# Half-empty operands moved from the streamed side to the loaded side of the matmuls, and a reordered start, in an attention-then-FFN kernel

## Chip, cores, metric

One core of a Trainium2 chip. The metric is the device time of one execution in microseconds (us). A profiled execution also has a span, from the first to the last instruction; it is about 1.7 us shorter than the time of that same execution (232.2 of 233.95 us before). The granted clock is the share of full rate at which PE was allowed to run.

PE is the matmul engine, PEld its weight loads, DVE the vector engine, ACT the scalar engine, POOL the GpSimd engine. A bank is one of the buffers in which PE leaves its sums; in this kernel DVE or ACT copies a sum out before its bank is used again. Silu is the activation h * sigmoid(h), done on ACT.

## The reference

Linear attention with decay over blocks, then a two-layer FFN with Silu. The inputs q, k, v are (4 batches, 8 heads, 768 positions, 64 dims), float32; the FFN is 512 to 2048 to 512 over 3072 tokens.

```python
for b in range(nb):                                   # blocks along the sequence
    intra = (qb @ kb^T) * Dmask;  intra = intra @ vb  # inside the block
    inter = (qb * lam_pow) @ kv_state                 # from all blocks before it
    out[block] = intra + inter
    kv_state = lam_block * kv_state + (kb * rev_pow)^T @ vb
x = out as tokens x 512
h = x @ w_in;  result = (h * sigmoid(h)) @ w_out
```

The kernel works in chunks of 128 positions (the reference's blocks have 64), 6 per batch, 24 in all; chunks 0, 6, 12 and 18 begin a batch and have no state.

## The kernel before

Two heads are packed in the 128 partitions (a "pair"; 4 pairs). A head has only 64 dims, so one operand of each product that contracts over dims must be zero for the other head. Before, the padded operand is the query, which streams through PE (`qt`, 256 columns per pair, half of them zeros).

```python
def st_t(c):                        # chunks 0 to 7: transposes on PE
    first = c < GROUPS[0] // BLK    # chunks 0 to 3
    tp = psum.tile([128, 2, NP, BLK], BF16, tag="o" if first else "att", ...)  # one bank for q and k
    ... 4 transposes of qb into tp[:, 0], 4 of kb into tp[:, 1] ...
    nc.vector.tensor_copy(qt[0:64, :, 0, :], tp[0:64, 0, :, :])
    nc.vector.tensor_copy(qt[64:128, :, 1, :], tp[64:128, 0, :, :])
    kt = tp[:, 1]                   # on ACT if first, else on DVE

def st_d(c):                        # state update
    vcast(c)                        # ACT: v to bf16
    ... 4 matmuls of 128 columns into kv; one 128x512 copy kv -> kvs ...

def st_s(c):                        # scores
    for half in range(2):
        for j in range(2):          # 256 streamed columns a pair
            nc.tensor.matmul(sp[:, 2*j:2*j+2, :], lhsT=kt[:, p, :], rhs=qt[:, p, :, :], ...)
        nc.vector.tensor_tensor(ss, sp, mask, op=AL.mult)

def st_o(c):                        # outputs
    for half in range(2):
        op = psum.tile([128, 2, 2, BLK], F32, tag="att", bufs=3)
        for j in range(2):          # 256 columns for each product
            nc.tensor.matmul(op[:, j, :, :], lhsT=pair_of(vb, p), rhs=res[half][:, 2*j:2*j+2, :], ...)
            if blk > 0:
                nc.tensor.matmul(op[:, j, :, :], lhsT=kvb[c][:, p, :], rhs=qt[:, p, :, :], ...)
        # of each [128, 2 heads] product only the two diagonal 64-row parts are wanted
        nc.scalar.activation(xt[g][0:64, ps, csl], op[0:64, :, 0, :], AF.Copy)
        nc.scalar.activation(xt[g][64:128, ps, csl], op[64:128, :, 1, :], AF.Copy)
```

So an output costs ACT four copies of 64x256, 0.38 us each in the trace. `ffn1(g, m)` is four matmuls of a group's columns into one of two `h` banks, which a Silu on ACT then empties; `ffn2` multiplies by `w_out`. After the start, `stretch(...)` interleaves `ffn1` tiles, `ffn2` parts and the pieces `t`, `d`, `s`, `o` of later chunks in a fixed order. One queue loads everything in order: chunks 0 to 3, `w_in` parts 0 to 3, chunk 4, `w_in` part 4, chunk 5, `w_out` parts. Each weight part is cast to bf16 on DVE before use.

## Time and profile before

| what | before |
|---|---|
| time, median of 3 (first measurement) | 234.6 us |
| span of the profiled run (its time: 233.95 us) | 232.2 us |
| PE busy | 209.8 us (90%) |
| ACT / DVE busy | 117.9 us (51%) / 81.3 us (35%) |
| start of the first output copy (DVE, `ob`) | 57.52 us |

The page of before: its heads, the busy time of each engine (us, share of the span, instructions), and the engines' shares of the chain that ended last.

```profile
span 232.2 us, 3510 instructions
...
PE 209.8 (90%) x1320; PEld 123.5 (53%) x1320; DVE 81.3 (35%) x130; ACT 117.9 (51%) x257; POOL 54.3 (23%) x60
...
PE 83%; ACT 7%; DVE 5%; issue 2%; DMA 1%; POOL 1%; ACTq 0%
```

PE bounds the kernel overall (90% of the span, 83% of the chain). Where it is back to back, time is the sum of the streamed columns: four products of 128, 256, 384 and 512 columns take 0.22, 0.44, 0.65 and 0.87 us in this trace. The timeline of before around one chunk's outputs (start us, length us, engine, line, operation, out<-in, partitions x elements, count):

```profile
119.44 0.27 PE L268 MATMUL op<-ss,vb 128*128 128x256 bf16 x1
119.54 0.27 PE L271 MATMUL op<-qt,kvs 128*128 128x256 bf16 x1
...
120.20 0.27 PE L271 MATMUL op<-qt,kvs 128*128 128x256 bf16 x1
120.31 0.81 PE L293 MATMUL h_ps<-xt,w_in_bf 128*128 128x384 bf16 x4
```

Read starts, not lengths: each of these products is 0.27 us long, but they start 0.10 to 0.11 us apart. The eight output products of 256 columns take 120.31 - 119.44 = 0.87 us.

The waits of PE in before, longest in total first (what waited, for what, total us, times, longest us):

```profile
PE tp L209 <- POOL qb L174: 6.7, 1, 6.7
PE sp L248 <- ACT kt L217: 4.1, 4, 1.6
PE kv_ps L232 <- ACT vb L191: 2.6, 3, 1.2
PE h_ps L293 <- ACT g L297: 1.9, 4, 0.7
```

In the start, scores wait for the key copy and the state update for the cast of v, both on ACT. Chunk 3 shows it, and what follows it:

```profile
21.47 0.61 PE L248 MATMUL sp<-qbd_99,kt 128*128 128x256 bf16 x4 [0.77 <-ACT kt L217]
...
23.29 0.38 PE L232 MATMUL kv_ps<-vb,kb 128*128 128x128 bf16 x4 [1.21 <-ACT vb L191]
...
27.43 7.93 PE L293 MATMUL h_ps<-xt,w_in_bf 128*128 128x512 bf16 x36 [0.25 <-ACT g L297]
```

The brackets give the idle time before and what ended it. On DVE, the cast of the last `w_in` part waits 5.03 us for its load, which lands at 33.7 us:

```profile
33.74 1.23 DVE L145 CAST w_in_bf<-w_tmp 128x2048 bf16<-128x2048 f32 x1 [5.03 <-DMA w_tmp<-in_moe_w_in_dram]
```

### The profile page before, as it was taken

To read this page: it belongs to the slowest core of one execution; us is meant where nothing else is said; L and a number is where in the kernel's file an instruction comes from. 1 tells how busy PE (TensorE), PEld (TensorE's weight loads), DVE (VectorE), ACT (ScalarE), POOL (GpSimd) and SP (SyncE) were. 2 spreads that over 40 slices of the span, in tenths; PEclk is the share of its full clock that TensorE was granted. 3 is DMA by queue.
4 is the path that set the end of the run, shared out by engine and by line. 5 is a ranking of instruction groups with operands and counts; after the bars stand their busy time and mean duration, and the time that the engine had idled before them with its cause. 6 is when DMAs were issued, how large, how long until landed. Compare 5 with 4: busy or idle time off the path is not lost.

```text
span 232.2 us, 3510 instructions
## 1 busy us (share of the span) xinstructions
PE 209.8 (90%) x1320; PEld 123.5 (53%) x1320; DVE 81.3 (35%) x130; ACT 117.9 (51%) x257; POOL 54.3 (23%) x60
## 2 busy tenths in 40 slices
PE   0465898899999988999999999999999999999993
PEld 0343545466555776666566555565666554444441
DVE  5378615740147533243224412430443310111121
ACT  5457665564403688567465554665466553433000
POOL 7661123025411223333333330333000000000000
PEclk9999999999999999999999999999999999999999
DMA  6999999999939998999999997999640100110212
GB/s 125 219 221 363 291 288 303 387 249 219 214 122 187 236 238 156 202 217 153 241 248 205 204 225 127 217 197 209 103 101 24 49 12 33 45 45 3 92 45 90
DMA packets 108849, 40.08 MB, mean 173 GB/s; under 512 B 101152, under 2 KB 102176, under 8 KB 108832
## 3 DMA queue, kind: packets, MB, share of 16 engines
q1 hardware_dynamic: 108688, 39.86, 77.4%
q8 instruction: 10, 0.16, 0.3%
q14 instruction: 7, 0.06, 0.1%
q10 hardware_dynamic: 144, 0.00, 0.0%
HBM read 27.27 MB, written 6.29 MB: 144 GB/s over the span
## 4 chain that ended last, share of the span: by engine, by line
PE 83%; ACT 7%; DVE 5%; issue 2%; DMA 1%; POOL 1%; ACTq 0%
PE o_ps L308 35%; PE h_ps L293 34%; PE sp L248 4%; PE op L268 4%; PE op L271 3%; PE kv_ps L232 2%; ACT xt L279 2%; ACT xt L278 2%; DMA lam_sb<-in_lam_dram 1%; ACT vb L191 1%; ACT kt L217 1%; PE tp L211 1%; ACT g L297 1%; DVE ss L251 1%; PE tp L209 1%
## 5 line engine op out<-in xcount | busy, mean ns | idle before, releaser
L293 PE MATMUL h_ps<-xt,w_in_bf 128*128 128x384 bf16 (+2 forms) x520 | 98.9, 323 | 2.6 <-ACT g L297 1.9
L297 ACT ACTIVATE g<-h_ps 128x384 bf16<-128x384 f32 (+2 forms) x128 | 62.3, 490 | 69.1 <-PE h_ps L293 68.2
L308 PE MATMUL o_ps<-w_out_bf,g 128*128 128x512 bf16 x384 | 94.9, 379 | 0.5 <-DVE w_out_bf L145 0.5
L293 PEld LDWEIGHTS <-w_in_bf 128*128 128x128 bf16 x520 | 50.3, 98 | 37.4 <-issue 3.9
L308 PEld LDWEIGHTS <-g 128*128 128x128 bf16 x384 | 37.3, 98 | 36.2 <-issue 0.7
L312 DVE COPY ob<-o_ps 128x512 f32<-128x512 f32 x24 | 16.6, 691 | 82.5 <-PE o_ps L308 82.5
L251 DVE TENSOR_TENSOR ss<-sp,mask 128x512 bf16<-128x512 f32 x48 | 30.9, 686 | 22.2 <-PE sp L248 22.0
L183 POOL TENSOR_TENSOR kb<-kf,lam_bwd 128x512 bf16<-128x512 f32 x24 | 25.0, 1042 | 4.2 <-DMA kf<-in_k_dram 2.4
L278 ACT ACTIVATE xt<-op 64x256 bf16<-64x256 f32 x44 | 16.5, 375 | 17.8 <-PE op L271 8.7
L268 PE MATMUL op<-ss,vb 128*128 128x256 bf16 x96 | 21.6, 277 | 0.2
L238 DVE CAST kvs<-kv_ps 128x512 bf16<-128x512 f32 x16 | 11.0, 688 | 24.7 <-PE kv_ps L232 24.7
L279 ACT ACTIVATE xt<-op 64x256 bf16<-64x256 f32 x44 | 16.6, 378 | 0.5
L174 POOL TENSOR_TENSOR qb<-qf,lam_fwd 128x512 bf16<-128x512 f32 x8 | 8.9, 1109 | 33.7 <-DMA qf<-in_q_dram 32.8
L248 PEld LDWEIGHTS <-kt 128*128 128x128 bf16 x96 | 8.8, 99 | 11.5 <-ACT kt L217 5.3
L191 ACT ACTIVATE vb<-vf 128x512 bf16<-128x512 f32 x24 | 14.8, 622 | 0.1
L271 PE MATMUL op<-qt,kvs 128*128 128x256 bf16 x56 | 13.1, 272 | 0.0
L177 POOL TENSOR_TENSOR qpad_107<-qf,lam_fwd 128x512 bf16<-128x512 f32 x5 | 5.2, 1042 | 27.1 <-DMA qf<-in_q_dram 23.3
L268 PEld LDWEIGHTS <-vb 128*128 128x128 bf16 x96 | 9.5, 100 | 2.9 <-issue 0.3
L177 POOL TENSOR_TENSOR qpad_109<-qf,lam_fwd 128x512 bf16<-128x512 f32 x6 | 6.3, 1042 | 20.0 <-DMA qf<-in_q_dram 12.6
L177 POOL TENSOR_TENSOR qpad_105<-qf,lam_fwd 128x512 bf16<-128x512 f32 x5 | 5.2, 1042 | 22.4 <-DMA qf<-in_q_dram 19.4
L232 PE MATMUL kv_ps<-vb,kb 128*128 128x128 bf16 x80 | 8.0, 223 | 2.6 <-ACT vb L191 2.6
L209 PE MATMUL tp<-ident,qb 128*128 128x128 bf16 x32 | 3.6, 242 | 6.7 <-POOL qb L174 6.7
(51 smaller groups left out, 82.4 us busy)
## 6 DMA issues: line engine op xcount, KB each, us to landing
qf<-in_q_dram SPq DMA_DIRECT2D x24, 256.0 KB, 3.7
kf<-in_k_dram SPq DMA_DIRECT2D x24, 256.0 KB, 4.3
vf<-in_v_dram SPq DMA_DIRECT2D x24, 256.0 KB, 4.5
out_dram<-ob SPq DMA_DIRECT2D x24, 256.0 KB, 2.3
w_tmp<-in_moe_w_out_dram SPq DMA_DIRECT2D x4, 1024.0 KB, 9.9
w_tmp<-in_moe_w_in_dram SPq DMA_DIRECT2D x3, 1024.0 KB, 7.8
w_tmp<-in_moe_w_in_dram SPq DMA_DIRECT2D x2, 512.0 KB, 5.5
kt<-kb SPq DMA_TRANSPOSE x16, 2.9
```

Source lines behind the costliest of these rows:

```text
L177: nc.gpsimd.tensor_tensor(qb[:, :, 0:4:3, :], qf.rearrange("s (p j) d -> s p j d", j=2), lam_fwd[:, blk, :].rearrange("s (p j) -> s p j", ...
L183: nc.gpsimd.tensor_tensor(kb, kf, lam_bwd[:, blk, :][:, :, None].to_broadcast([128, H, D]), op=AL.mult)
L191: nc.scalar.activation(natb[c][2], vraw.pop(c), AF.Copy)
L248: nc.tensor.matmul(sp[:, 2 * j:2 * j + 2, :], lhsT=kt[:, p, :], rhs=qt[:, p, :, :], start=True, stop=True)
L251: nc.vector.tensor_tensor(ss, sp, mask[:, None, :].to_broadcast([128, 4, BLK]), op=AL.mult)
L268: nc.tensor.matmul(op[:, j, :, :], lhsT=pair_of(vb, p), rhs=res[half][:, 2 * j:2 * j + 2, :], start=True, stop=(blk == 0))
L271: nc.tensor.matmul(op[:, j, :, :], lhsT=kvb[c][:, p, :], rhs=qt[:, p, :, :], start=False, stop=True)
L278: nc.scalar.activation(xt[g][0:64, ps, csl], op[0:64, :, 0, :], AF.Copy)
L279: nc.scalar.activation(xt[g][64:128, ps, csl], op[64:128, :, 1, :], AF.Copy)
L293: nc.tensor.matmul(hp[:, a:z], lhsT=w_in_bf[:, ko, m * 128:(m + 1) * 128], rhs=xt[g][:, ko, a:z], start=(ko == 0 and a == 0), stop=(ko == ...
L297: nc.scalar.activation(gg, hp[:, :n], AF.Silu)
L308: nc.tensor.matmul(o, lhsT=gt[g, ko][:, mt * BLK:(mt + 1) * BLK], rhs=w_out_bf[:, ko, :], start=(ko == 0), stop=(ko == KO_OUT - 1))
```

## The change

The intent: pad the operand that is loaded as weights, not the one that streams. Values (`vpad`), keys (`ktbd`) and the state (`kvbd`) get zeroed halves, four buffers of each, cleared once; the query is dense. Then the state product of a pair needs 128 columns for both heads, all products of an output add up in one bank, and one copy takes it out. Scores go by even and odd heads to two banks. For the first four chunks, query and key transposes get banks of their own, so that ACT copies the query while DVE copies the key. Casts of v are issued ahead of the scores. (On PE the first chunks' transposes already stood ahead of the outputs of the chunk before.)

```diff
@@ scores: same columns, other split
-        for half in range(2):
-            for j in range(2):
-                nc.tensor.matmul(sp[:, 2*j:2*j+2, :], lhsT=kt[:, p, :], rhs=qt[:, p, :, :], ...)
+        for j in range(2):
+            for p in range(NP):
+                nc.tensor.matmul(sp[:, p, :], lhsT=kt[:, p, j, :], rhs=qt[:, p, :], start=True, stop=True)
@@ outputs: 8 x 256 columns become 12 x 128, one bank, one copy
+        op = psum.tile([128, NP, BLK], F32, tag="att", bufs=3)
+        terms = [(kvb[c][:, p, :], qt[:, p, :], p) for p in range(NP)] if blk > 0 else []
+        for j in range(2):
+            terms += [(vb[:, p, 2*j:2*j+2, :], res[j][:, p, :], p) for p in range(NP)]
+        for i, (lhsT, rhs, p) in enumerate(terms):
+            nc.tensor.matmul(op[:, p, :], lhsT=lhsT, rhs=rhs, start=(i == 0), ...)
+        if c < N0:                                   # chunks 0 to 3
+            nc.scalar.activation(xt[g][:, 0:2, csl], op[:, 0:2, :], AF.Copy)
+            nc.vector.tensor_copy(xt[g][:, 2:4, csl], op[:, 2:4, :])
+        else:
+            nc.scalar.activation(xt[g][:, :, csl], op, AF.Copy)
@@ state: two half copies into the padded tile (ACT for chunks 0 to 3, else DVE)
-        nc.vector.tensor_copy(kvs, kv)
+        for j in range(2):
+            half_copy(nc.scalar if c < N0 else nc.vector, ...)   # 64x256 each
@@ keys of later chunks arrive dense by transposing DMA, then two DVE copies spread them
+    def spread_k(c): ...
@@ start
-    for c in range(4):
-        prep(c); st_t(c)
-        if c > 0: st_o(c - 1)
-        if c == 3: cast_w("in", 0)
-        st_s(c), st_d(c)
-    cast_w("in", 1)
-    ffn1(0, 0, 0), ffn1(0, 1, 0); st_o(3)
-    ffn1(0, 0, 1), ffn1(0, 1, 1); cast_w("in", 2); ...; ffn1(0, 2), ffn1(0, 3)
+    for c in range(N0):
+        prep(c); st_tq(c); st_tk(c)                  # own banks: tags "o" and "h"
+        if c > 0: st_o(c - 1)
+        vcast(c)
+        if c == N0 - 1: cast_w("in", 0)
+        st_s(c)
+        if c == N0 - 1: cast_w("in", 1)
+        st_d(c)
+    ffn1(0, 0, 0), ffn1(0, 1, 0); st_o(N0 - 1)
+    ffn1(0, 2, 0, tag="o"), ffn1(0, 3, 0, tag="o")
+    for m in range(4): ffn1(0, m, 1)
@@ ... chunks 4 and 5: transposes, casts and tiles slightly reordered; w_out casts in two halves (cut)
```

More of the change, by code (lines that the diff above doesn't have):

```diff
@@ L75, with clear @@
     )
-    NQBD = 3
-    qbd, qpad = [], []
-    for i in range(NQBD):
-        t = const.tile([128, NP, 2, BLK], BF16, name=f"qbd{i}")
-        nc.vector.memset(t, 0.0)
-        qbd.append(t)
-    for i in range(NQBD):
-        t = const.tile([128, NP, 4, D], BF16, name=f"qpad{i}")
-        nc.gpsimd.memset(t, 0.0)
-        qpad.append(t)
+    NKV = 4
+    vpad, ktbd, kvbd = [], [], []
+    for i in range(NKV):
+        vpad.append(const.tile([128, NP, 4, D], BF16, name=f"vpad{i}"))
+        ktbd.append(const.tile([128, NP, 2, BLK], BF16, name=f"ktbd{i}"))
+        kvbd.append(const.tile([128, NP, BLK], BF16, name=f"kvbd{i}"))
+    def clear(i):
+        nc.vector.memset(vpad[i], 0.0)
+        nc.vector.memset(ktbd[i], 0.0)
+        nc.vector.memset(kvbd[i], 0.0)
     log_lam = const.tile([128, H], F32)
@@ L92 @@
     nc.vector.tensor_copy(iota_f, iota_i)
+    clear(0)
+    clear(1)
     lam_exp = const.tile([128, NB, H], F32)
@@ L99 @@
     )
+    clear(2)
+    clear(3)
     lam_fwd = const.tile([128, NB, H], F32)
@@ L140, in cast_w @@
             dst = w_out_bf[:, a:z, :]
-        if which == "in" and i < 2:
+        if which == "in" and i == 0:
             nc.vector.tensor_copy(dst[:, 0:2, :], t[:, 0:2, :])
             nc.scalar.activation(dst[:, 2:4, :], t[:, 2:4, :], AF.Copy)
-        else:
-            nc.vector.tensor_copy(dst, t)
+        elif which == "in":
+            nc.vector.tensor_copy(dst, t)
+        else:
+            nc.vector.tensor_copy(dst[:, 0:2, :], t[:, 0:2, :])
+            nc.vector.tensor_copy(dst[:, 2:4, :], t[:, 2:4, :])
     raw, natb, tr, st, kvb, kvps = {}, {}, {}, {}, {}, {}
@@ L156 @@
     xt = {}
+    N0 = GROUPS[0] // BLK
     def load_c(c):
@@ L167, in load_c, with decay @@
         raw[c] = (qf, kf, vf)
+    def decay(table, blk):
+        return table[:, blk, :].rearrange("s (p j) -> s p j", j=2)[:, :, :, None].to_broadcast([128, NP, 2, D])
     def prep(c):
@@ L171, in prep @@
         qf, kf, vf = raw.pop(c)
-        if c < NPET:
-            qb = nat.tile([128, H, D], BF16, tag="qb")
-            nc.gpsimd.tensor_tensor(qb, qf, lam_fwd[:, blk, :][:, :, None].to_broadcast([128, H, D]), op=AL.mult)
-        else:
-            qb = qpad[c % NQBD]
-            nc.gpsimd.tensor_tensor(
-                qb[:, :, 0:4:3, :], qf.rearrange("s (p j) d -> s p j d", j=2),
-                lam_fwd[:, blk, :].rearrange("s (p j) -> s p j", j=2)[:, :, :, None].to_broadcast([128, NP, 2, D]),
-                op=AL.mult)
-        kb = nat.tile([128, H, D], BF16, tag="kb")
-        vb = nat.tile([128, H, D], BF16, tag="vb")
-        nc.gpsimd.tensor_tensor(kb, kf, lam_bwd[:, blk, :][:, :, None].to_broadcast([128, H, D]), op=AL.mult)
+        qb = nat.tile([128, NP, 2, D], BF16, tag="qb")
+        nc.gpsimd.tensor_tensor(qb, qf.rearrange("s (p j) d -> s p j d", j=2), decay(lam_fwd, blk), op=AL.mult)
+        kb = nat.tile([128, NP, 2, D], BF16, tag="kb")
+        nc.gpsimd.tensor_tensor(kb, kf.rearrange("s (p j) d -> s p j d", j=2), decay(lam_bwd, blk), op=AL.mult)
         vraw[c] = vf
-        natb[c] = (qb, kb, vb)
+        natb[c] = (qb, kb, vpad[c % NKV])
     vraw = {}
@@ L190, in vcast @@
         if c in vraw:
-            nc.scalar.activation(natb[c][2], vraw.pop(c), AF.Copy)
+            nc.scalar.activation(natb[c][2][:, :, 0:4:3, :],
+                                 vraw.pop(c).rearrange("s (p j) d -> s p j d", j=2), AF.Copy)
     def dma_t(c):
         qb, kb, vb = natb[c]
-        kt = work.tile([128, NP, BLK], BF16, tag="kt")
-        qt = nat.tile([128, NP, 2, BLK], BF16, tag="qt")
-        nc.sync.dma_start_transpose(qt.rearrange("d p j s -> d (p j) s"), qb.rearrange("s p x d -> s (p x d)"))
@@ L198, in dma_t @@
-        nc.sync.dma_start_transpose(kt, kb.rearrange("s h d -> s (h d)"))
-        tr[c] = (qt, kt)
-    def pair_of(t, p):
-        return t[:, 2 * p:2 * p + 2, :]
+        qt = nat.tile([128, NP, BLK], BF16, tag="qt")
+        kn = nat.tile([128, NP, BLK], BF16, tag="kn")
+        nc.sync.dma_start_transpose(qt, qb.rearrange("s p j d -> s (p j d)"))
+        nc.sync.dma_start_transpose(kn, kb.rearrange("s p j d -> s (p j d)"))
+        tr[c] = (qt, ktbd[c % NKV])
+        knat[c] = kn
+    knat = {}
@@ new lines, in spread_k, with half_copy, st_tq @@
+    def spread_k(c):
+        if c in knat:
+            kn, kt = knat.pop(c), ktbd[c % NKV]
+            for j in range(2):
+                half_copy(nc.vector, lambda sl, j: kt[sl, :, j, :], lambda sl, j: kn[sl, :, :], j)
+    def half_copy(eng, dst, src, j):
+        sl = slice(64 * j, 64 * j + 64)
+        if eng is nc.scalar:
+            nc.scalar.activation(dst(sl, j), src(sl, j), AF.Copy)
+        else:
+            nc.vector.tensor_copy(dst(sl, j), src(sl, j))
+    def st_tq(c):
+        qb, kb, vb = natb[c]
+        tp = psum.tile([128, NP, BLK], BF16, name="tq", tag="o", bufs=2, padded_shape=[128, 2 * NP, BLK])
+        for p in range(NP):
+            nc.tensor.transpose(tp[:, p, :], qb[:, p, :, :], ident)
+        qt = nat.tile([128, NP, BLK], BF16, tag="qt")
+        nc.scalar.activation(qt, tp, AF.Copy)
+        tr[c] = (qt, ktbd[c % NKV])
@@ L204, in st_t, with st_tk @@
+    def st_tk(c):
+        qb, kb, vb = natb[c]
+        tp = psum.tile([128, NP, BLK], BF16, name="tk", tag="h", bufs=2, padded_shape=[128, 2 * NP, BLK])
+        for p in range(NP):
+            nc.tensor.transpose(tp[:, p, :], kb[:, p, :, :], ident)
+        kt = ktbd[c % NKV]
+        for j in range(2):
+            half_copy(nc.vector, lambda sl, j: kt[sl, :, j, :], lambda sl, j: tp[sl, :, :], j)
     def st_t(c):
         qb, kb, vb = natb[c]
-        first = c < GROUPS[0] // BLK
-        tp = psum.tile([128, 2, NP, BLK], BF16, name="tp", tag="o" if first else "att", bufs=2 if first else 3)
+        tp = psum.tile([128, 2, NP, BLK], BF16, name="tp", tag="att", bufs=3)
@@ L208, in st_t @@
         for p in range(NP):
-            nc.tensor.transpose(tp[:, 0, p, :], pair_of(qb, p), ident)
+            nc.tensor.transpose(tp[:, 0, p, :], qb[:, p, :, :], ident)
         for p in range(NP):
-            nc.tensor.transpose(tp[:, 1, p, :], pair_of(kb, p), ident)
-        qt = qbd[c % NQBD]
-        kt = work.tile([128, NP, BLK], BF16, tag="kt")
-        nc.vector.tensor_copy(qt[0:64, :, 0, :], tp[0:64, 0, :, :])
-        nc.vector.tensor_copy(qt[64:128, :, 1, :], tp[64:128, 0, :, :])
@@ L216, in st_t @@
-        if first:
-            nc.scalar.activation(kt, tp[:, 1, :, :], AF.Copy)
-        else:
-            nc.vector.tensor_copy(kt, tp[:, 1, :, :])
+            nc.tensor.transpose(tp[:, 1, p, :], kb[:, p, :, :], ident)
+        qt = nat.tile([128, NP, BLK], BF16, tag="qt")
+        kt = ktbd[c % NKV]
+        nc.vector.tensor_copy(qt, tp[:, 0, :, :])
+        for j in range(2):
+            half_copy(nc.vector, lambda sl, j: kt[sl, :, j, :], lambda sl, j: tp[sl, 1, :, :], j)
         tr[c] = (qt, kt)
@@ L231, in st_d @@
         for p in range(NP):
-            nc.tensor.matmul(kv[:, p, :], lhsT=pair_of(kb, p), rhs=pair_of(vb, p),
+            nc.tensor.matmul(kv[:, p, :], lhsT=kb[:, p, :, :], rhs=vb[:, p, 0:4:3, :],
                              start=(blk == 0 and p == 0), stop=True, skip_group_check=True)
-        kvs = work.tile([128, NP, BLK], BF16, tag="kvs")
-        if c < GROUPS[0] // BLK:
-            nc.scalar.activation(kvs, kv, AF.Copy)
-        else:
-            nc.vector.tensor_copy(kvs, kv)
+        kvs = kvbd[c % NKV]
+        for j in range(2):
+            half_copy(nc.scalar if c < N0 else nc.vector,
+                      lambda sl, j: kvs[sl, :, 64 * j:64 * j + 64], lambda sl, j: kv[sl, :, 64 * j:64 * j + 64], j)
         kvb[c + 1] = kvs
     def st_s(c):
+        spread_k(c)
         qt, kt = tr[c]
         res = []
-        for half in range(2):
-            sp = psum.tile([128, 4, BLK], F32, tag="att", bufs=3)
-            for j in range(2):
-                p = 2 * half + j
-                nc.tensor.matmul(sp[:, 2 * j:2 * j + 2, :], lhsT=kt[:, p, :], rhs=qt[:, p, :, :],
-                                 start=True, stop=True)
+        for j in range(2):
+            sp = psum.tile([128, NP, BLK], F32, tag="att", bufs=3)
+            for p in range(NP):
+                nc.tensor.matmul(sp[:, p, :], lhsT=kt[:, p, j, :], rhs=qt[:, p, :], start=True, stop=True)
             ss = work.tile([128, 4, BLK], BF16, tag="ss")
@@ L263, in st_o, with ffn1 @@
         csl = slice(off * BLK, (off + 1) * BLK)
-        for half in range(2):
-            op = psum.tile([128, 2, 2, BLK], F32, tag="att", bufs=3)
-            for j in range(2):
-                p = 2 * half + j
-                nc.tensor.matmul(op[:, j, :, :], lhsT=pair_of(vb, p), rhs=res[half][:, 2 * j:2 * j + 2, :],
-                                 start=True, stop=(blk == 0))
-                if blk > 0:
-                    nc.tensor.matmul(op[:, j, :, :], lhsT=kvb[c][:, p, :], rhs=qt[:, p, :, :],
-                                     start=False, stop=True)
-            ps = slice(2 * half, 2 * half + 2)
-            if c < GROUPS[0] // BLK and half == 1:
-                nc.vector.tensor_copy(xt[g][0:64, ps, csl], op[0:64, :, 0, :])
-                nc.vector.tensor_copy(xt[g][64:128, ps, csl], op[64:128, :, 1, :])
-            else:
-                nc.scalar.activation(xt[g][0:64, ps, csl], op[0:64, :, 0, :], AF.Copy)
-                nc.scalar.activation(xt[g][64:128, ps, csl], op[64:128, :, 1, :], AF.Copy)
+        op = psum.tile([128, NP, BLK], F32, tag="att", bufs=3)
+        terms = [(kvb[c][:, p, :], qt[:, p, :], p) for p in range(NP)] if blk > 0 else []
+        for j in range(2):
+            terms += [(vb[:, p, 2 * j:2 * j + 2, :], res[j][:, p, :], p) for p in range(NP)]
+        for i, (lhsT, rhs, p) in enumerate(terms):
+            nc.tensor.matmul(op[:, p, :], lhsT=lhsT, rhs=rhs, start=(i == 0), stop=(i >= len(terms) - NP),
+                             skip_group_check=True)
+        if c < N0:
+            nc.scalar.activation(xt[g][:, 0:2, csl], op[:, 0:2, :], AF.Copy)
+            nc.vector.tensor_copy(xt[g][:, 2:4, csl], op[:, 2:4, :])
+        else:
+            nc.scalar.activation(xt[g][:, :, csl], op, AF.Copy)
     gt = {}
     hps = {}
-    def ffn1(g, m, part=None):
+    def ffn1(g, m, part=None, tag="h"):
         n = GROUPS[g]
@@ L289, in ffn1 @@
         if a == 0:
-            hps[g, m] = psum.tile([128, 512], F32, name="h_ps", tag="h", bufs=2)
+            hps[g, m] = psum.tile([128, 512], F32, name="h_ps", tag=tag, bufs=2)
         hp = hps[g, m]
@@ L328 @@
     load_w("out", 0)
-    for c in range(4):
+    for c in range(N0):
         prep(c)
-        st_t(c)
+        st_tq(c)
+        st_tk(c)
         if c > 0:
             st_o(c - 1)
-        if c == 3:
+        vcast(c)
+        if c == N0 - 1:
             cast_w("in", 0)
-        st_s(c), st_d(c)
-    cast_w("in", 1)
+        st_s(c)
+        if c == N0 - 1:
+            cast_w("in", 1)
+        st_d(c)
     ffn1(0, 0, 0), ffn1(0, 1, 0)
-    st_o(3)
-    ffn1(0, 0, 1), ffn1(0, 1, 1)
+    st_o(N0 - 1)
+    ffn1(0, 2, 0, tag="o"), ffn1(0, 3, 0, tag="o")
+    for m in range(4):
+        ffn1(0, m, 1)
     cast_w("in", 2)
     load_w("out", 1)
-    ffn1(0, 2), ffn1(0, 3)
     prep(4)
@@ L350 @@
         ffn1(0, m)
+    for m in range(8, 11):
+        ffn1(0, m)
+    vcast(4)
+    st_t(4)
     cast_w("in", 4)
-    for m in range(8, 12):
-        ffn1(0, m)
-        if m == 10:
-            st_t(4)
+    ffn1(0, 11)
     load_w("out", 3)
@@ L359 @@
     ffn1(0, 12)
+    st_o(4)
     ffn1(0, 13)
-    st_o(4)
     ffn1(0, 14)
+    vcast(5)
     st_t(5)
+    cast_w("out", 0)
     ffn1(0, 15)
-    cast_w("out", 0)
     st_s(5), st_d(5)
@@ L393, in piece @@
             vcast(c + 1)
+        if kind == "o":
+            spread_k(c + 1)
     def ups(g):
```

## The prediction

> What bounds the kernel now. The page gives PE 209.8 us busy of a 232.2 us span (90%); the chain of waits is 83% PE. From about 47 us on, the timeline shows matmuls back to back: four of 512 columns take 0.87 us, four of 256 take 0.44, four of 128 take 0.22 (217, 109 and 55 ns each). There the time is the sum of streamed columns. Before 47 us the table by stretches shows 9.7 us of PE work in 6.7-23.5 us, and the timeline later waits (0.55, 0.53, 0.52 us): arriving data and short chains through ACT and DVE pace that part.
>
> Per chunk on PE. Scores: 4 x 256 columns become 8 x 128, the same. Outputs: 8 x 256 (the state products streamed half zeros, half of the value products was thrown away) become 12 x 128: 0.87 us becomes 12 x 55 = 0.66. So 0.2 us is saved in each chunk with a preceding state, nothing in the other 4 of 24. [...] eight transposes in a row, each with its own load, take 0.45 us, 56 ns each. I go with the trace. Chunks 7 to 23 hold 15 such chunks: 3.0 us, all on the critical path.
>
> Other engines. ACT loses four 64x256 copies (1.5 us) for one of 128x512 (0.6). DVE gains: state in two halves (0.84 for 0.69), two spreading copies per chunk from 8 on. Both have room (35% and 51% busy): off the critical path. The 12 clears (about 5 us on DVE) mostly sit in the wait for lam and the table load. A small loss: in chunks 6 and 7 the state copies stand ahead of the masks and outputs follow closely: 0.4 us.
>
> The start. Loads pace it: chunk 3's kb is ready at 18.0 us, whatever PE does. Before, its scores started at 21.5 and the first group's ffn1 tiles 0 and 1 were done at 27.4. Now query copies go to ACT and key copies to DVE at once, value casts come ahead of the scores; I expect these scores at about 19.5 us, and tiles 0 to 3 (1.7 us more work) done near 25.2: 4 us ahead. But the last w_in part lands at 33.7 us (its DVE cast waited 5.0 us). The faster PE runs into that: about 1 us idle before tile 12, then short waits, since the masks of chunk 4 stand behind this cast on DVE and those of chunk 5 behind the first w_out cast (landing near 40.2, estimated from the last at 49.2 and 3.0 us each). I put the end of the second ffn2 piece at 44.0 us instead of 47.3: 3.3 us gained.
>
> Sum: 3.3 + 3.0 - 0.4 = 5.9 us, 234.6 to 228.7 us.
>
> What would show it: 12 output matmuls at 55-56 ns; no PE wait for DVE or ACT after 75 us; PE busy down 3-4 us; chunk 3's scores near 19.5 us; a new wait of PE on the w_in cast at 33-35 us; back-to-back work from 44 us; ACT busy down 17 us.
>
> What would make it wrong: weight loads not hidden over 12 to 20 matmuls in a row, or a cost of accumulating in one bank (to 230-231); DVE copies ahead of masks stalling PE in each chunk; spreading copies that wait for their DMA; the start gaining less. Better: the weights land earlier.
>
> Chances: faster by over 2%: 0.82; within 2%: 0.16; slower: 0.02. Range 226.8 to 230.4.

(The 12 clears took 4.97 us on DVE in after, eight of 0.485 us and four of 0.272, and the table loads 1.28 us each on ACT in both traces.)

## More of the kernel before

The fourth row of the waits (PE for Silu results `g`) is easy to pass over at 1.9 us. Its place is the stretch from 78 to 92 us, here on PE:

```profile
83.29 0.60 PE L293 MATMUL h_ps<-xt,w_in_bf 128*128 128x256 bf16 x4 [0.56 <-ACT g L297]
...
87.52 0.60 PE L293 MATMUL h_ps<-xt,w_in_bf 128*128 128x256 bf16 x4 [0.35 <-ACT g L297]
...
91.91 1.25 PE L293 MATMUL h_ps<-xt,w_in_bf 128*128 128x256 bf16 x8 [0.72 <-ACT g L297]
```

and here on ACT, where four output copies stand ahead of the Silu that frees the `h` bank:

```profile
81.28 0.38 ACT L278 ACTIVATE xt<-op 64x256 bf16<-64x256 f32 x1
81.67 0.38 ACT L279 ACTIVATE xt<-op 64x256 bf16<-64x256 f32 x1
82.06 0.38 ACT L278 ACTIVATE xt<-op 64x256 bf16<-64x256 f32 x1
82.45 0.38 ACT L279 ACTIVATE xt<-op 64x256 bf16<-64x256 f32 x1
82.85 0.66 ACT L297 ACTIVATE g<-h_ps 128x256 bf16<-128x256 f32 x2
```

## The result, and the profile after

| what | before | after |
|---|---|---|
| time, median of 4 | 234.58 us (234.56 to 234.6) | 228.88 us (228.68 to 229.34) |
| ratio | | 0.976 (95%: 0.9743 to 0.9777) |
| span of the profiled run (its time) | 232.2 us (233.95 us) | 227.0 us (228.68 us) |
| PE busy | 209.8 us | 206.7 us |
| ACT / DVE busy | 117.9 / 81.3 us | 98.4 / 94.9 us |

A ratio here is the mean time of one kernel's runs over that of the other's runs of the same rounds, so it is not quite the ratio of the medians quoted. The change is faster by more than 2%, and 228.9 lies 0.2 us from the predicted 228.7. The rest of this text asks whether it came from where the prediction said.

The same views of after. The page:

```profile
span 227.0 us, 3875 instructions
...
PE 206.7 (91%) x1496; PEld 125.1 (55%) x1520; DVE 94.9 (42%) x187; ACT 98.4 (43%) x196; POOL 51.2 (23%) x57
...
PE 72%; SPq 14%; DVE 7%; DMA 3%; issue 2%; ACT 0%; DVEq 0%
```

The loading queue (SPq, DMA) is now in the chain that ended last, and ACT has left it. One chunk's outputs:

```profile
122.44 0.39 PE L302 MATMUL op<-qt,kvbd_107 128*128 128x128 bf16 x4
122.66 0.61 PE L302 MATMUL op<-ss,vpad_108 128*128 128x128 bf16 x8
123.11 0.81 PE L322 MATMUL h_ps<-xt,w_in_bf 128*128 128x384 bf16 x4
```

Twelve products take 123.11 - 122.44 = 0.67 us, 56 ns each, where before eight took 0.87. The waits of PE:

```profile
PE tq L228 <- POOL qb L186: 6.7, 1, 6.7
PE h_ps L322 <- DVE w_in_bf L151: 2.7, 2, 1.4
PE tk L237 <- POOL kb L188: 1.7, 3, 0.8
PE op L302 <- DVE ss L283: 1.2, 5, 0.4
PE o_ps L337 <- DVE w_out_bf L153: 0.8, 1, 0.8
```

No wait for Silu is left, the waits for the key copy on ACT are gone, and the waits for weight casts and for masks (`ss`) are new. The start, and the cast of the last `w_in` part on DVE:

```profile
19.04 0.86 PE L281 MATMUL sp<-qt,ktbd_109 128*128 128x128 bf16 x8
20.19 0.38 PE L266 MATMUL kv_ps<-vpad_108,kb 128*128 128x128 bf16 x4 [0.29 <-ACT vpad_108 L196]
...
26.46 6.22 PE L322 MATMUL h_ps<-xt,w_in_bf 128*128 128x512 bf16 x27 [1.28 <-DVE w_in_bf L151]
...
36.47 0.81 PE L322 MATMUL h_ps<-xt,w_in_bf 128*128 128x512 bf16 x3 [1.43 <-DVE w_in_bf L151]
```

```profile
34.96 1.23 DVE L151 CAST w_in_bf<-w_tmp 128x2048 bf16<-128x2048 f32 x1 [0.59 <-DMA w_tmp<-in_moe_w_in_dram]
```

Chunk 3's scores are 2.4 us earlier; the first four `ffn1` tiles are done at about 25.2 us, as predicted; then PE waits twice for weight casts. (A count below a multiple of four, such as x27, means matmul records missing from the trace.) In the stretch that held waits for Silu before, PE now waits for masks once:

```profile
83.05 0.38 PE L302 MATMUL op<-ss,vpad_102 128*128 128x128 bf16 x4 [0.39 <-DVE ss L283]
83.64 0.38 PE L302 MATMUL op<-ss,vpad_102 128*128 128x128 bf16 x4 [0.21 <-DVE ss L283]
```

### Where the 5.2 us went

The 24 output copies (`ob` on DVE) stand in the same order in both kernels, so their starts cut both traces at the same points of the work. Copies 1, 6, 7 and 20 in before, then in after:

```profile
57.52 0.69 DVE L312 COPY ob<-o_ps 128x512 f32<-128x512 f32 x1 [7.07 <-PE o_ps L308]
78.38 0.69 DVE L312 COPY ob<-o_ps 128x512 f32<-128x512 f32 x1 [2.41 <-PE o_ps L308]
102.64 0.68 DVE L312 COPY ob<-o_ps 128x512 f32<-128x512 f32 x1
213.83 0.69 DVE L312 COPY ob<-o_ps 128x512 f32<-128x512 f32 x1 [7.08 <-PE o_ps L308]
...
55.58 0.69 DVE L341 COPY ob<-o_ps 128x512 f32<-128x512 f32 x1 [3.90 <-PE o_ps L337]
76.66 0.69 DVE L341 COPY ob<-o_ps 128x512 f32<-128x512 f32 x1 [1.42 <-PE o_ps L337]
99.28 0.68 DVE L341 COPY ob<-o_ps 128x512 f32<-128x512 f32 x1
208.57 0.69 DVE L341 COPY ob<-o_ps 128x512 f32<-128x512 f32 x1 [7.08 <-PE o_ps L337]
```

The segments, worked out as differences of those starts (copies 1, 6, 7, 20, 24):

| segment | before | after | gain | predicted |
|---|---|---|---|---|
| start, to copy 1 | 57.52 | 55.58 | 1.94 | 3.3 (at a mark 10 us earlier) |
| copies 1 to 6 (chunks 6, 7) | 20.86 | 21.08 | -0.22 | 0.2 - 0.4 = -0.2 |
| copies 6 to 7 (chunks 8 to 11) | 24.26 | 22.62 | 1.64 | 4 x 0.2 = 0.8 |
| copies 7 to 20 (chunks 12 to 23) | 111.19 | 109.29 | 1.90 | 10 x 0.2 = 2.0 |
| copies 20 to 24 | 14.67 | 14.68 | -0.01 | 0 |
| sum | 228.50 | 223.25 | 5.25 | 5.9 |

By the traces the gain is 5.25 us; by the medians it is 5.7. The profiled run of before was 0.6 us faster than its median, and no profile of a 234.6 us run is on record, so the missing 0.45 us cannot be placed. The total was nearly right because two errors pulled opposite ways: the start gave 1.4 us less, the third segment 0.8 us more. The segments are worth using: except for the start and the third one, they repeat within 0.1 us in every run of the same code below, while times of whole runs scatter by 1 to 2 us. The third varies between 22.1 and 22.6 us in after. The start varies most: after's start order was traced eight times in all (in after, in its variants and in two more executions named below), and its first output copy came between 55.47 and 58.18 us. So the 1.94 us of the start are the difference of two single draws.

### The profile page after: what moved, and what is told of

Its sections match the earlier page's. It is cut to its first block, busy times and chain, and to the rows that moved or that the text cites. A ratio compares the mean times of both kernels' runs of the same rounds, so it can differ in the third digit from the quotient of the medians. Undisturbed runs are those within 1.5% of the kernel's fastest.

```text
span 227.0 us, 3875 instructions
## 1 busy us (share of the span) xinstructions
PE 206.7 (91%) x1496; PEld 125.1 (55%) x1520; DVE 94.9 (42%) x187; ACT 98.4 (43%) x196; POOL 51.2 (23%) x57
## 2 busy tenths in 40 slices
DMA packets 100659, 38.02 MB, mean 167 GB/s; under 512 B 92960, under 2 KB 93984, under 8 KB 100640
## 4 chain that ended last, share of the span: by engine, by line
PE 72%; SPq 14%; DVE 7%; DMA 3%; issue 2%; ACT 0%; DVEq 0%
PE o_ps L337 34%; PE h_ps L322 29%; SPq L176 6%; SPq L175 5%; PE op L302 5%; DMA w_tmp<-in_moe_w_out_dram 3%; PE sp L281 3%; DVE ss L283 3%; SPq L174 2%; SPq L136 2%; PE kv_ps L266 1%; DVE ob L341 1%; DVE ktbd_103 L221 1%; DVE kvbd_110 L221 0%; DVE kvbd_107 L221 0%
## 5 line engine op out<-in xcount | busy, mean ns | idle before, releaser
L337 PE MATMUL o_ps<-w_out_bf,g 128*128 128x512 bf16 x364 | 91.8, 379 | 1.9 <-DVE w_out_bf L153 0.8
L186 POOL TENSOR_TENSOR qb<-qf,lam_fwd 128x512 bf16<-128x512 f32 x24 | 25.1, 1048 | 104.2 <-DMA qf<-in_q_dram 95.5
L308 ACT ACTIVATE xt<-op 128x512 bf16<-128x512 f32 x20 | 11.9, 597 | 24.7 <-PE op L302 24.6
L266 PEld LDWEIGHTS <-kb 128*128 128x128 bf16 x80 | 6.3, 102 | 3.3 <-issue 1.1
L221 DVE CAST kvbd_101<-kv_ps 64x256 bf16<-64x256 f32 x10 | 4.2, 421 | 6.3 <-PE kv_ps L266 6.2
L221 DVE CAST kvbd_107<-kv_ps 64x256 bf16<-64x256 f32 x10 | 4.2, 421 | 4.7 <-PE kv_ps L266 4.6
L151 DVE CAST w_in_bf<-w_tmp 128x2048 bf16<-128x2048 f32 (+1 forms) x4 | 4.4, 1090 | 4.1 <-DMA w_tmp<-in_moe_w_in_dram 4.1
L281 PE MATMUL sp<-qt,ktbd_100 128*128 128x128 bf16 x48 | 4.3, 234 | 0.6 <-DVE ktbd_100 L221 0.5
L302 PE MATMUL op<-ss,vpad_102 128*128 128x128 bf16 x48 | 4.0, 218 | 0.8 <-DVE ss L283 0.8
L221 DVE CAST kvbd_104<-kv_ps 64x256 bf16<-64x256 f32 x6 | 2.5, 422 | 4.6 <-PE kv_ps L266 4.5
L281 PEld LDWEIGHTS <-ktbd_100 128*128 128x128 bf16 x48 | 3.3, 104 | 2.0 <-DVE ktbd_100 L221 1.5
L153 DVE CAST w_out_bf<-w_tmp 128x1024 bf16<-128x1024 f32 x4 | 2.8, 694 | 3.8 <-DMA w_tmp<-in_moe_w_out_dram 3.8
L281 PE MATMUL sp<-qt,ktbd_103 128*128 128x128 bf16 x48 | 4.3, 235 | 0.1
```

The costliest lines, as they stand in the source:

```text
L186: nc.gpsimd.tensor_tensor(qb, qf.rearrange("s (p j) d -> s p j d", j=2), decay(lam_fwd, blk), op=AL.mult)
L221: nc.vector.tensor_copy(dst(sl, j), src(sl, j))
L281: nc.tensor.matmul(sp[:, p, :], lhsT=kt[:, p, j, :], rhs=qt[:, p, :], start=True, stop=True)
L302: nc.tensor.matmul(op[:, p, :], lhsT=lhsT, rhs=rhs, start=(i == 0), stop=(i >= len(terms) - NP), skip_group_check=True)
L308: nc.scalar.activation(xt[g][:, :, csl], op, AF.Copy)
L337: nc.tensor.matmul(o, lhsT=gt[g, ko][:, mt * BLK:(mt + 1) * BLK], rhs=w_out_bf[:, ko, :], start=(ko == 0), stop=(ko == KO_OUT - 1))
```

## The experiments

Three chips, each kernel with 5 rounds beside before unless noted. The median of before was 235.15, 235.16 and 234.62 us in them. After was run again: 228.60 us (227.27 to 229.93, 6 runs). Ratios are to before of the same call. Only the runs (after again, state copies on ACT, scores first, both orders) had after beside them; the times of the others are set against after on another chip, so their segments weigh more than their medians.

### Output copies in four pieces again

```diff
-            nc.scalar.activation(xt[g][:, :, csl], op, AF.Copy)
+            for ps in (slice(0, 2), slice(2, 4)):
+                for sl in (slice(0, 64), slice(64, 128)):
+                    nc.scalar.activation(xt[g][sl, ps, csl], op[sl, ps, :], AF.Copy)
```

> After, with each later chunk's output copied out by four 64x256 ACT copies (about 1.5 us) again instead of one 128x512 copy (0.6 us). Theory A (part of the gain came from ACT: before, PE waited 1.6 us between 82 and 92 us for Silu results because ACT was held by these copies): these PE waits for ACT come back, 0.8 to 1.6 us slower than after, about 229.7 to 230.5 us. Rival B (my prediction: the gain after 47 us is the streamed columns alone, ACT is off the critical path): within 0.3 us of after, 228.9 us.

Measured: 231.85 us (231.0 to 233.16), ratio 0.9868. The waits of PE from 76 to 105 us:

```profile
PE h_ps L324 <- ACT g L328: 3.1, 3, 1.2
PE op L302 <- DVE ss L283: 0.4, 2, 0.2
```

The segment of chunks 8 to 11 grew from 22.62 to 25.17 us, all later segments stayed (109.30 and 14.67). The start of this run was 1.5 us later too (57.10), with the load of the last `w_in` part landing at 35.7 us, so not all of the 3 us in time belongs to the copies. The segment does: it is 2.55 us longer with nothing but ACT work added. Theory A stands, and its size was underrated; rival B, the prediction's claim, falls.

### Before, with half of the copies on DVE

```diff
-            if c < GROUPS[0] // BLK and half == 1:
+            if half == 1:
                 nc.vector.tensor_copy(xt[g][0:64, ps, csl], op[0:64, :, 0, :])
```

> The kernel before, with the second half of each later chunk's output copies on DVE instead of ACT, no other change. Theory A (ACT held PE up between 82 and 92 us, 1.6 us): the PE waits for Silu there vanish or fall under 0.4 us, some waits for masks on DVE may come instead; 0.8 to 1.6 us faster than before. Rival B (ACT is off the critical path): within 0.3 us of before.

Measured: 233.39 us (232.48 to 234.94) beside 234.62, ratio 0.993 (0.9897 to 0.9964). In the same window the only wait of PE is

```profile
PE sp L248 <- DVE kt L219: 0.6, 1, 0.6
```

and the segment of chunks 8 to 11 fell from 24.26 to 22.35 us, a gain of 1.9 us without removing one column. The other later segments are those of before (20.95, 111.19, 14.67). So ACT alone was worth 1.9 us there, and the change's merged copy got it as a side effect. In time the gain was 1.2 us; the three of its runs at full clock (0.998 to 1.0) took 232.48 to 233.04 us, those of before in this call 234.57 to 234.62, which makes 1.5 to 2.1 us. (Its profiled run had a stretch at half clock in the start, see below, so its start is not compared.) This run also answers a rival that the text has not named: the dense query makes the transposing loads of later chunks smaller (40.08 MB moved in before, 38.02 in after). Here all 40.08 MB are still moved, and chunks 8 to 11 are as fast as in after (22.12 and 22.62 us).

### The removed columns put back

```diff
+        again = NP if blk > 0 else 0
+        terms = terms[:again] + terms            # state products twice, the second set starts afresh
-            ... start=(i == 0), ...
+            ... start=(i in (0, again)), ...
```

> After, with the four state products of each chunk issued twice (the second set starts the sum afresh, so the result stays right): it puts back exactly the 512 streamed columns that the change removed, and nothing else. If the columns count in full where PE is back to back: 15 chunks x 4 x 55 ns = 3.3 us slower, 232.2 us; the 5 earlier chunks fall into waits for loads and add under 0.5 us. If the gain came mainly from fewer copies and shorter waits: under 1.5 us slower.

Measured: 230.75 us (229.9 to 233.27), ratio 0.9823; the result is right. Segments: start 55.92, then 21.08, 22.37, 111.52, 14.68. In chunks 12 to 23 the ten chunks with a state cost 111.52 - 109.29 = 2.23 us, 0.223 us each, which is 4 x 56 ns: the columns count in full. (This run moves only 38.02 MB, and is yet no faster there than before, 111.19 us: the smaller loads are worth nothing in that segment either.) In chunks 6 to 11 they cost next to nothing (21.08 us as in after; 22.37 us against 22.62 and 22.12 in two profiles of after), which fits that after waits for masks there (0.6 us from 76 to 105 us), so that extra state products fill idle time. Taken with the run before this one, which reaches 22.35 us in chunks 8 to 11 with all of before's columns, this says that the columns were worth nothing in that segment: its gain is ACT's. So the 3.3 us expected were an overestimate: 2.0 us show (span 229.3 less the start difference of 0.3, against 227.0).

### One bank for the first chunks' transposes again

```diff
-        tp = psum.tile([128, NP, BLK], BF16, name="tq", tag="o", ...)   # and "tk", tag "h"
+        tp = psum.tile([128, 2, NP, BLK], BF16, name="tq", tag="o", bufs=2)
         ... 8 transposes, then the two key copies on DVE, then the query copy on ACT ...
```

> After, with the query and key transposes of the first four chunks in one bank again (query copy after the key copies). Theory A (loads pace the start: PE waits 1.3 and 1.4 us for the w_in casts at 25 to 36 us, so the chain of the first chunks has slack): chunk 3's scores start 0.5 to 1.2 us later, the total stays within 0.3 us of after. Rival B (the own banks shorten a critical chain): 0.5 us or more slower.

Measured: 229.21 us (228.24 to 230.64), ratio 0.9757. Chunk 3's scores:

```profile
21.31 0.61 PE L280 MATMUL sp<-qt,ktbd 128*128 128x128 bf16 x8 [1.00 <-ACT qt L235]
```

They are 2.3 us later than in after, as late as in before, yet the span is 227.1 us (after 227.0) and the first output copy starts at 55.82 us (after 55.58). Only the waits for the weight casts shrank (from 2.7 to 1.0 us). The own banks, a named part of the change, do what they were meant to do, and gave no time that these runs show: PE waits for the loads' casts less instead.

### The whole start put back

The bank as above, and the casts of v after the scores, and the first tiles in the old order:

```diff
-        vcast(c)
-        if c == N0 - 1: cast_w("in", 0)
-        st_s(c)
-        if c == N0 - 1: cast_w("in", 1)
-        st_d(c)
+        if c == N0 - 1: cast_w("in", 0)
+        st_s(c), st_d(c)
+    cast_w("in", 1)
     ffn1(0, 0, 0), ffn1(0, 1, 0); st_o(N0 - 1)
-    ffn1(0, 2, 0, tag="o"), ffn1(0, 3, 0, tag="o")
-    for m in range(4): ffn1(0, m, 1)
+    ffn1(0, 0, 1), ffn1(0, 1, 1); cast_w("in", 2); ...; ffn1(0, 2), ffn1(0, 3)
```

> After, with the whole start put back: one bank for the first chunks' transposes, value casts after the scores, the first tiles of ffn1 in the old order. Everything from chunk 4 on stays as changed. Theory A (the start as a whole is worth about 1.9 us at the first output copy, of which the own banks alone gave nothing): tile 4 starts near 28.5 to 29.2 us instead of 26.5, the first output copy is at 56.6 to 57.5 us instead of 55.5, 1.0 to 2.0 us slower than after. Rival B (the loads pace everything up to 45 us, so the start order is worth nothing): within 0.5 us of after.

Measured: 229.23 us (228.38 to 230.12), ratio 0.9748; span 227.8; first output copy at 56.67 us. Tile 4 started near 28.3 us (26.52 us plus eight products of 0.217 us), a little before the expected 28.5 to 29.2. Set against the first trace of after, this start is 1.1 us slower, at the low end of theory A and above rival B's limit. But 56.67 us lies inside the 55.47 to 58.18 us of after's own start order, and in time the difference to after (228.60 and 228.88) is 0.35 to 0.6 us, below the scatter of these runs: what this part of the start order is worth stays open. The remaining 0.85 us between 56.67 and before's 57.52 may lie in the parts of chunks 4 and 5 that were not put back (their transposes, casts and outputs) or in the draw; no run took them singly.

### The last part of w_in not loaded

```diff
-    for i in range(5): load_w("in", i) ...        # cast of part 4 reads part 3's tile: wrong on purpose
+    for i in range(4): load_w("in", i)
```

> After, with the last part of w_in not loaded (its cast reads the part before it; the result is wrong on purpose): 1 MB less ahead of the first w_out part. Theory A (the last loads pace the stretch from 33 to 45 us): the waits of PE for the w_in cast at 35 us (1.4 us) and for the w_out cast at 42 us (0.8 us) go, 1.8 to 2.8 us faster, 226.1 to 227.1 us. Rival B (the stretch is paced by the chains through DVE and ACT): under 0.7 us faster.

Measured: 227.14 us (227.05 to 227.22), ratio 0.9659; the result is wrong. The first output copy is at 54.59 us, 1.0 us earlier than in after; the span is 225.4. Better than rival B and short of theory A. The trace says why: the cast of part 4 now waits for no load, but it starts only at 34.31 us, because it stands behind chunk 4's key copies on DVE, and still takes 1.35 us in one piece. PE's waits for the `w_in` casts fell from 2.7 to 2.0 us, those for the `w_out` cast from 0.8 to 0.3. So the late load holds some of PE's wait at 36 us in after; that the DVE order and the undivided cast share the rest is the author's reading, and no run took them singly.

### After again, before again: the landing of the loads

Both unchanged; before with one look only.

> The changed kernel itself, on this chip beside the others, and a second profile of it. Theory A (the later landing of the w_in parts, 35.0 us where before had 33.7, belongs to this kernel or to the draw of a run): ratio 0.976 again; if the second profile again has the cast of the last w_in part at 34.5 us or later, the delay goes with the kernel, if it has it near 33.7 it was chance.

> The kernel before, unchanged, for a second profile. If the later landing of the w_in parts goes with the changed kernel, the cast of the last w_in part again ends its wait near 33.7 us; if it is the draw of a run, it is anywhere between 33.5 and 35.5 us. PE waits for Silu between 82 and 92 us again 1.3 to 1.9 us.

After again: ratio 0.9722, first output copy at 55.47 us, cast of the last `w_in` part at 34.39 us after a wait for its load. In this run the third segment is 22.12 us instead of 22.62, with waits for masks of 0.2 us at most: the mask wait of 0.39 us in the first profile is not in every run.

Before again: the cast starts at 34.09 us. With the run with copies on DVE (34.19) that makes 33.7, 34.1 and 34.2 us in three traces of the old start, and 34.2 to 35.7 us in the nine traces of the changed kernel and its variants in which this cast waited for its load. The ranges touch; the load tends to land later in the changed kernel, mostly by under 1 us, and why stays open.

The second profile of before shows something else. Its time was 235.77 us, and its first output copy came at 59.33 us, not 57.52, while all its later segments repeat (20.85, 24.27, 111.19). Its stretches of the start, with the granted clock in the column before the DMA share:

```profile
20.00:23.00 3.00, 1.91 (x20) 1.29 (x18) 2.79 (x7) 2.15 (x5) 0.00 (x0) 1.00 1.06 388
23.00:26.00 3.00, 2.11 (x16) 1.68 (x16) 1.32 (x3) 1.95 (x4) 0.00 (x0) 0.77 1.07 370
26.00:29.00 3.00, 2.62 (x14) 1.53 (x13) 1.70 (x3) 1.17 (x3) 0.92 (x1) 0.66 1.35 227
```

(The five busy times are those of PE, PEld, DVE, ACT and POOL.) The clock was halved from 24.6 to 28.1 us, 3.4 us long, worked out from the shares 0.77 and 0.66; PE's products of 256 columns start 0.21 us apart from 25.3 to 26.8 us, where they have 0.11 us from 20.3 to 21.0 us. In the 3.4 us before it PE was not idle, but had little work: it was busy 1.44 us, and its longest wait was 1.21 us. Why the clock fell was not shown. The halved stretch is not the whole delay. PE's products of 256 columns had also come to the shorter spacing later: until 17.7 us they start 0.21 us apart, where the first profile has 0.11 us from 15.9 us on, and chunk 3's scores were already 0.6 us late (22.07 us). The clock column shows 1.00 there in both traces, so it does not show this difference.

A stretch like this fits the two times of before: 18 of its 33 runs took 235.09 to 236.21 us, every one with a mean granted clock of 0.989 to 0.993, and the other 15 took 233.95 to 234.62 us, every one at 0.998 or 1.0. Of the ten runs of after only one had 0.993 (229.34 us). The four runs of before first compared with after (234.56 to 234.6 us) show no sign of it, so the 2.4% contains no such effect; the larger gains in later ratios contain some.

The changed kernel is not free of it. A second trace of after again is of another execution (span 229.2 us, where the one read above has 226.4). There the last `w_in` part landed at 36.4 us, PE waited 2.54 us for its cast, the clock was then halved from 38.3 to 41.7 us, and the first output copy came at 58.18 us. A second trace of the run below with state copies on ACT (span 227.8 us, where the one read there has 226.4) has such a stretch from 44.2 to 47.6 us, after a wait of PE of 1.70 us for the first `w_out` cast, and the profile of before with half of the copies on DVE one from 24.5 to 27.9 us. In the 3.4 us before them PE was busy 0.88, 1.64 and 1.44 us. So in two traces of the changed kernel a stretch at half clock followed PE's wait for a late load; that the one brought the other was not shown.

### State copies on ACT

```diff
-            half_copy(nc.scalar if c < N0 else nc.vector, ...)
+            half_copy(nc.scalar, ...)
```

> After, with the two state copies of each later chunk on ACT instead of DVE. Theory A (state copies ahead of the masks on DVE make PE wait for masks, 1.2 us in all in after): the PE waits for masks fall under 0.4 us, but ACT is short in the stretch from 76 to 92 us, so some waits for Silu come back there; the sum within 0.6 us of after, either way. Rival B (ACT has room everywhere since it lost 0.9 us per chunk): 0.6 us or more faster than after.

Measured: 227.87 us (226.99 to 228.46), ratio 0.9684; after 228.60 us and 0.9722. PE waits for masks fell to 0.2 us and none for Silu came back. The segment of chunks 6 and 7 fell from 21.08 to 20.31 us; that of chunks 8 to 11 is 22.12, as in after's second run. By the segments a gain of 0.77 us (20.32 us in a second trace of it), so rival B's number is met, and theory A's cause is confirmed with it: state copies ahead of the masks cost those 0.77 us. My fear that ACT would be short again was wrong. By time, 0.7 us, with intervals that overlap.

### Scores first, and both orders

Scores before the state update from chunk 8 on:

```diff
-    ... else ("d", "s", "o"))]
+    ... else ("s", "d", "o"))]
```

> After, with the scores of each chunk from 8 on issued before its state update, so that the masks stand before the state copies on DVE and outputs follow two places later. Theory A: the PE waits for masks between 76 and 92 us (0.6 us) vanish, those of chunks 5 to 7 stay: 0.4 to 0.8 us faster than after. Rival B (the waits only move to the scores' own operands): no gain, within 0.2 us.

Measured: 230.31 us (228.53 to 230.77), ratio 0.979, slower than after. A wait of 0.7 us of PE for the spread keys (`ktbd`) appeared between 57 and 105 us, where after has none: the scores now follow too closely on the copies that make their own operand. Rival B was right about the mechanism. The third segment (22.17) and the next (109.39) of its profile explain no loss beyond 0.1 us; the profiled run took 228.53 us and the five others 230.2 or more, without a trace. What slowed those stays open.

The start order changed further, on top of scores first:

```diff
-        elif which == "in": nc.vector.tensor_copy(dst, t)      # all but part 0 now in two halves
     ffn1(0, 12)
-    st_o(4); ffn1(0, 13); ffn1(0, 14)
-    vcast(5); st_t(5); cast_w("out", 0)
-    ffn1(0, 15); st_s(5), st_d(5); ffn2(0, 0, range(0, 4)); st_o(5)
+    ffn1(0, 13); st_o(4)
+    vcast(5); st_t(5); ffn1(0, 14)
+    st_s(5), st_d(5); ffn1(0, 15); st_o(5)
+    cast_w("out", 0); ffn2(0, 0, range(0, 4))
```

> After, with scores first (as in the run beside it) and the start reordered: w_in casts in two halves, tile 13 before chunk 4's outputs, masks and outputs of chunk 5 before the first w_out cast. Theory A (at the start PE waits for casts that stand behind loads, and could do other work there): 1.3 us at the start and 0.6 us later, 1.4 to 2.2 us faster than after, about 227 us. Rival B (all work before 42 us is bound by the loads, order does not matter): under 0.8 us.

Measured: 228.02 us (227.71 to 229.15), ratio 0.9709. The first output copy is at 54.32 us, 1.15 us earlier than in after of the same call: both traces of this start order (this one and the next section's) lie below all eight of after's, so order does matter within the load-bound start. Scores first gave 1.1 us back in chunks 8 to 11 (23.25 us against 22.12), again in waits for `ktbd` (1.6 us).

### The version that the runs point to

The start order of the last run, state copies on ACT, no scores first.

> The best version that the runs point to: after, with the start order of the run with both orders (its first output copy came 1.2 us earlier) and the state copies on ACT (0.7 us less between chunks 6 and 7), without scores first. If both add up: 1.5 to 2.0 us faster than after, about 226.8 us in the median. If the earlier start brings the waits for Silu back or the loads absorb it: under 1.0 us faster.

Measured: 226.91 us (225.17 to 227.97), ratio 0.9661 (0.9632 to 0.9689), result right. Its profiled run has a span of 223.4 us, the first output copy at 53.24 us, and segments of 20.32, 22.17, 109.29 and 14.67 us. Between 57 and 105 us its waits list is empty. It beats both kernels. Against after it is 1.7 to 2.0 us in the medians (228.60 and 228.88), taken on other chips; the full-clock runs of before agree within 0.7 us over those chips, so most of that should be real, and the ratios to before (0.9661 against 0.9722 and 0.976) point the same way. The segments of its profile against those of after's second profile give the parts: 2.2 us at the start (of which about 0.2 is an earlier load) and 0.76 us in chunks 6 and 7. That profile is of the fastest of the six runs, 1.7 us under their median, so part of its start may be a lucky draw.

## Why the prediction was right, and where it was not

**Columns: right where PE is back to back.** "12 output matmuls at 55-56 ns" and 0.2 us per chunk with a state; measured 0.67 us for twelve, and 1.90 us over the ten chunks from 12 on, 0.19 each. Putting the columns back cost 0.223 us each there. The term rested on the trace of before alone, where eight transposes with a load each take 0.45 us, 56 ns each. But "15 such chunks: 3.0 us, all on the critical path" held for ten of them: in chunks 7 to 11 the columns put back cost nothing, so about 1.0 us of the 3.0 was not to be had from columns.

**Chunks 6 and 7: right cause, right net by luck.** Predicted -0.2 net (0.2 from columns, 0.4 lost to state copies ahead of the masks), measured -0.22. State copies on ACT removed that cause and gave 0.77 us, twice the predicted loss, and the columns gave nothing there; what made up the other 0.55 us no run shows.

**"Both have room (35% and 51% busy): off the critical path": this step failed, for ACT.** A mean over the run was taken for a stage. From 77.5 to 92.2 us ACT was busy 11.66 of 14.7 us (79%), with two `h` banks and runs of four copies of 0.38 us between Silus. PE waited 1.6 us there in before. Two runs show it from both sides: half the copies off ACT in before gave 1.9 us in that segment, four copies in after cost 2.55 us. Of the third segment's 1.64 us gain 4 x 0.2 = 0.8 was predicted, and from the columns; by these two runs and the one with the columns put back (22.37 us), all of it came from ACT, net of new mask waits. One copy of 512 columns took 597 ns on ACT in after, one of 256 columns 375 to 378 ns in before, so that one takes 0.60 us where four took 1.5; why half the columns do not take half the time was not shown.

**The start: right mechanism, mis-sized.** Chunk 3's scores at 19.5 us predicted, 19.04 measured; tiles 0 to 3 done at 25.2 predicted and measured; a wait for the cast near 33 to 35 us predicted, 1.43 us up to 36.5 measured. The end of the second `ffn2` piece was put at 44.0 us and came at 45.6, so 1.65 us were gained there and not 3.3. The terms that were off: the last `w_in` part landed at 35.0 us (34.4 in the second profile), not 33.7; its cast ran in one piece; the first `w_out` part landed at 41.9 us, not 40.2, for 0.8 us of waiting; and PE waited 1.28 us for `w_in` part 2 before tile 4, which the text did not foresee. "The start gaining less" stood among what could go wrong. Since the start of one and the same code varied by 2.7 us between traces, part of this miss may be the draw.

**"No PE wait for DVE or ACT after 75 us": wrong in the first profile** (0.6 us for masks of chunk 9); in the second the waits were smaller (0.6 us in all from 57 us on, none over 0.2 us).

**The sum** held by luck: the third segment gave 0.8 us more than predicted, from ACT and not from columns, the start 1.4 us less, and the median of before lay 0.6 us above the profiled run from which the prediction was worked out. Of the other signs, PE busy fell by 3.1 us (3 to 4 predicted) and ACT busy by 19.5 (17 predicted).

## What to carry to other kernels

When an operand must be half zeros, put the zeros in the operand that is loaded as weights, as long as 128-column products with a load each run at about 56 ns in the trace at hand: streamed columns are what PE paid for here (twelve such products took 0.67 us, and four put back cost 0.223 us a chunk). Before calling an engine off the critical path, read its busy share and PE's waits for it stage by stage; here 51% on average hid a stretch at 79% that held PE up by 1.6 us. The same holds for a gain in columns: it paid in the ten chunks where PE was back to back, and not in the five where PE waited. Where loads pace a stage, shortening a compute chain in it may give nothing (the own banks here: a span of 227.1 us without them, 227.0 with them) until other ready work is moved into the waits (the first output copy then came at 54.32 us instead of 55.47). And before a start is compared by one trace, trace the same code again.
